# Decay attention with two MLPs on one core: W_out's bounds from VectorE maxima, filler products on TensorE, and a new table of priorities

## The chip, the cores and the metric

The kernel runs on one core of a Trainium2 chip. The metric is the device time of that core in microseconds (us). Engines go by these names: PE is TensorE's matrix products and PEld its weight loads, DVE is VectorE, ACT is ScalarE, POOL is GpSimd, and SP is the queue that issues the DMAs.

## The reference

Three layers follow one another. Attention: 4 batches, 8 heads, 576 positions, head size 64.

```python
scores = scale * (q @ k.T) + cum[:, None] - cum[None, :]   # cum = cumsum(log(clip(f)))
attn = softmax(causal(scores)); x = attn @ v               # then (2304, 512)
x = relu(x @ w_in) ** 2 @ w_out                            # moe: d_ff 2048
out = (silu(x @ w_gate) * (x @ w_val)) @ w_out2            # moe2: d_ff 1536
```

The weights come as 64-bit floats, so each 512-column block of W_in or W_out is 2 MB and is converted on the chip.

## The kernel before

**Staging.** The first 256 rows of each batch ("early") are worked through for all 16 head pairs; batches 0 and 1 keep their products in fp32 on PE (scores L792, transposition L869, mix with V L933). As soon as batch 0 has its eight pieces of x (ACT L968, then DVE L973), the first MLP starts on this tile: `h<-x,i` (L1141) are the products with W_in, `acc<-g,o` (L1209) those with W_out. The first layer of two tiles is done ahead (384 products L1141) before the first L1209. The rest of attention (f16, L945) and the first MLP then interleave; the second MLP (L1404, L1520) closes the program.

**A weight block** (`stage`) is loaded by SP (L362), two ACT operations take its high and low words (L369, L372), DVE joins them (L377). Then a bound is needed from which a power of two is made as its scale. For W_in and W_out (`nm in "io"`) PE multiplies every 128x128 piece of the block with itself (`gram`, L398; 16 products for a block) and DVE takes the row maxima of the sum (`norm`, L403). For the other weights DVE takes the largest magnitude of each piece (`extent`, L406). `scale_of` and `top` spread the largest value over the partitions by PE (L315, L324) and DVE (L319, L294 to L300). With the scale, `split` writes f16 high and low parts (ACT L457, DVE L461). `tables1` (DVE L1085 to L1093) needs the scales of all eight blocks; the squares (ACT L1170) need `tables1`; then come the f16 high part (ACT L1184), the low part (POOL L1187) and the first L1209.

**The order.** Every piece of work is a `Step` with a priority. `Plan.order` puts the steps on a planned clock, per engine always the ready one with the lowest priority number whose buffers are free; the order that it finds is the program order of each engine, so every engine then runs its own list strictly in order. Priorities of the early attention units (`EPRI`), of the batches' V (`VPRI`), of the weight blocks and of their loads (`IPRI`, `ILOAD`, `OPRI`, `OLOAD`), of the second MLP's weights (`GPRI`, `GATE0`) and `FREE` (how many W_in loads don't wait for the first bias load) are tables of numbers. Two PSUM buffers ("hp", tag `h`) are shared by L1141's results, the `top` of V and small products.

Of the kernel before, what the change touches and what calls it, by code (L numbers as in the profile page):

```python
# [8 lines left out]
F32 = mybir.dt.float32  # L9
F32R = mybir.dt.float32r  # L10
F16 = mybir.dt.float16
BF16 = mybir.dt.bfloat16
# [6 lines left out]
PE, ACT, DVE, POOL, SP = "PE", "ACT", "DVE", "POOL", "SP"  # L19
AFTER = {PE: 0.25, ACT: 0.2, DVE: 0.15, POOL: 0.2, SP: 0.0, None: 0.0}  # L20
DMA_ISSUE = 0.45
QUEUE = 8
DMA_LATENCY = 1.8
DMA_RATE = 290e3
LAG1 = 3
# [31 lines left out]
class Plan:  # L57
# [9 lines left out]
    def add(self, eng, us, fn, deps=(), pri=0, take=(), use=(), nbytes=0, order=(), late=0.0):  # L67
        deps, order = ([d for d in ds if d is not None] for ds in (deps, order))
        st = Step(len(self.steps), eng, us, fn, deps, order, pri, take, nbytes)
        st.hot = getattr(fn, "__name__", "") in SHARED[eng] if eng in SHARED else False  # L70
        st.late = late
        for buf in (*take, *use):
            buf.users.append(st)
        self.steps.append(st)
        return st

    def order(self):
# [22 lines left out]
        while left:  # L100
            moved = False
            for e in free:
# [14 lines left out]
                if e == SP:  # L117
                    free[e] = now + st.us
                    if len(landed) >= QUEUE:
                        free[e] = max(free[e], landed[-QUEUE] + 0.1)  # L120
                    dma_free = max(free[e], dma_free) + st.nbytes / DMA_RATE
                    st.done = dma_free + DMA_LATENCY + st.late
                    landed.append(st.done)
# [39 lines left out]
    return 0.1 + n * 0.0021  # L163


GPRI = 900
GATE0 = -2
GATE = 5
EPRI = [-10, 30, 23, 50, 38, 100, 110, 16, 120, 12, 143, 334, 297, 334, 440, 437]
VPRI = [5, 90, 550, 178]  # L170
IPRI, ILOAD = [60, 65, 75, 41], [-15, -17, 10, 40]
OPRI, OLOAD = [128, 113, 177, 290], [115, 132, 180, 126]
VERBOSE = False
WHOLE = 2
SQUARE = 7
FREE = 2
COPY = (ACT, ACT)
ROUNDS = [(0, 1), (8,), (2, 3), (4, 5), (6, 7)]
LAST = ROUNDS[-1]
# [3 lines left out]
def decay_attention_moe_kernel(ctx: ExitStack, tc, q, k, v, f, w1, w2, wg, wv, wo, outT):  # L183
    nc = tc.nc
    P = 128
    B, H, _, S = q.shape
# [5 lines left out]
    NG1 = w1.shape[0]  # L192
    NG2 = wg.shape[0]
# [9 lines left out]
    HN = 2  # L203
# [15 lines left out]
    ps_h = ctx.enter_context(tc.tile_pool(name="ps_h", bufs=HN, space=bass.MemoryType.PSUM))  # L219
# [10 lines left out]
    add = plan.add  # L230
# [6 lines left out]
    def table(name, *shape, dt=F32):  # L237
        return small.tile([P, *shape], dt, tag=name, bufs=1, name=name)
# [3 lines left out]
    ones = table("ones", P, dt=BF16)  # L242
# [2 lines left out]
    XI, XS = table("xi", B + 1), table("xs", B + 1)  # L245
    KX = table("kx", 2, B * NP)
    FY = table("fy", B + 1)
    MT = table("mt", 2 * NG1 + 9 * NG2, dt=BF16)
    NSC = 2 * NG1 + 3 * NG2
    SWI, SWS = table("swi", NSC), table("sws", NSC)  # L250
    ISF, ISG, ISV = (SWI[:, 2 * NG1 + NG2 * n : 2 * NG1 + NG2 * n + NG2] for n in range(3))
# [36 lines left out]
    o3 = add(ACT, 2.0, lambda: nc.scalar.activation(fc[0], fc[0], AF.Ln), [o3], -10, use=[fc_buf])  # L288
    o3 = add(DVE, 1.9, fc_scan, [o3, o2], -10, use=[fc_buf])
    decayed = add(SP, DMA_ISSUE, lambda: nc.sync.dma_start(cum_d, fc[0]), [o3], -10, use=[fc_buf], nbytes=74000)  # L290

    def power(src, c, kk, inv, s, mask=0x7F800000):
        t = small.tile([P, 2], F32, tag="pw", bufs=4, name="pw")
# [54 lines left out]
    def stage(nm, u, places, pri, lpri, deps=(), gates=(), where="hp"):  # L348
        src = SRC[nm]
        c = {"key": (nm, u), "pri": pri, "pieces": [], "bufs": []}  # L350
        g_buf, g_bank = bank(where)
        col = COL[nm] + u
        joined = []
        k0 = 0
        for tag, nb, make, nk in places:
            buf, n = Buf(tag, nb), 512 * nk
            piece = {"ks": slice(k0, k0 + nk), "nk": nk}
            k0 += nk

            def load(piece=piece, make=make, nk=nk):  # L360
                raw = make()
                nc.sync.dma_start(raw.rearrange("p (k n) -> p k n", k=nk), src[u, :, piece["ks"], :].bitcast(I32))  # L362
                words = raw.rearrange("p (n t) -> p n t", t=2)
                piece["lo"], piece["hi"] = words[:, :, 0], words[:, :, 1]
                piece["b"] = raw.bitcast(BF16).rearrange("p (k n t) -> p k n t", k=nk, t=4)[:, :, :, 3]

            def top_half(piece=piece):
                t = piece["hi"].bitcast(F32)
                nc.scalar.activation(t, t, AF.Prelu, scale=2.0**-112, alpha=2.0**32)  # L369

            def low_half(piece=piece):
                nc.scalar.activation(  # L372
                    piece["lo"], piece["lo"].bitcast(U32), AF.Copy, bias=-0.49, scale=2.0**-29 * (1 - 2.0**-9)
                )

            def join(piece=piece):
                nc.vector.scalar_tensor_tensor(  # L377
                    piece["hi"], piece["hi"], 3, piece["lo"], op0=ALU.logical_shift_left, op1=ALU.bitwise_or
                )

            ld = chained(add(SP, DMA_ISSUE, load, deps, lpri + 0.1 * u, take=[buf], nbytes=WIDE * P * n * 8,
                             order=[prev(tag), *gates, *paced(nm), *came[-PACE[nm]:][:1]]), tag)
            s1 = add(ACT, 0.1 + act_us(n), top_half, [ld], pri, use=[buf])
            s2 = add(ACT, 0.1 + act_us(n), low_half, [ld], pri, use=[buf])
            came.append(s1)
            joined.append(add(DVE, dve_us(n), join, [s1, s2], pri, use=[buf]))
            c["pieces"].append(piece)
            c["bufs"].append(buf)
            c["load"] = ld

        def gram(piece):
            for kk in range(4)[piece["ks"]]:
                if kk == 0:
                    c["ps"] = g_bank()
                w = piece["b"][:, kk - piece["ks"].start, :]
                for n in range(4):
                    b = w[:, P * n : P * n + P]
                    nc.tensor.matmul(  # L398
                        c["ps"][:, 0:P], b, b, start=kk == 0 and n == 0, stop=kk == 3 and n == 3,
                    )  # L400

        def norm():
            nc.vector.tensor_reduce(MT[:, col : col + 1], c["ps"][:, 0:P], axis=mybir.AxisListType.X, op=ALU.max)  # L403

        def extent(piece, at):
            nc.vector.tensor_reduce(  # L406
                MT[:, at : at + 1], piece["hi"].bitcast(F32), axis=mybir.AxisListType.X, op=ALU.max,
                apply_absolute_value=True,
            )

        c["joined"] = joined
        if (nm, u) in PEEKED:
            pass
        elif nm in "io":
            st = None
            for piece, buf, jn in zip(c["pieces"], c["bufs"], joined):
                st = add(PE, 0.25 * piece["nk"], lambda piece=piece: gram(piece), [jn, st], pri,
                         take=() if st else [g_buf], use=[buf, *([g_buf] if st else ())])
            c["cols"] = (col, col + 1)
            c["stat"] = [add(DVE, 0.05 + dve_us(P), norm, [st], pri, use=[g_buf])]  # L420
        else:
            m0 = 2 * NG1 + 3 * (col - 2 * NG1)
            c["cols"] = (m0, m0 + len(places))
            c["stat"] = [
                add(DVE, dve_us(512 * piece["nk"]), lambda piece=piece, at=m0 + n: extent(piece, at), [jn], pri, use=[buf])
                for n, (piece, buf, jn) in enumerate(zip(c["pieces"], c["bufs"], joined))
            ]
        return c

    def scale_of(nm, u, c, pri, where="hp"):  # L430
        idx = COL[nm] + u
        kk, mask = (13, 0x7F000000) if nm == "o" else (13 if nm in "gv" else 14, 0x7F800000)
        lo, hi = c["cols"]
        whole = 1 if nm in "io" else 512
        return top(
            lambda: MT[:, lo:hi], hi - lo, c["stat"], pri,
            lambda ps: power(ps, VSCALE * 1.02 * whole, kk, SWI[:, idx : idx + 1], SWS[:, idx : idx + 1], mask), 0.9,
            where=where, square=whole > 1,
        )
# [558 lines left out]

    def own_scale(nm, u, places, pri=GPRI, lpri=GPRI - 5, deps=(), gates=(), where="hp"):
        c = stage(nm, u, places, pri, lpri, deps=deps, gates=gates, where=where)  # L1000
# [15 lines left out]
    def peek(nm, u, places):  # L1016
# [3 lines left out]
        for n, (tag, nb, make, nk) in enumerate(places):  # L1020
# [7 lines left out]
            def extent(n=n):  # L1028
                if "t" not in cell:
# [6 lines left out]

            ld = chained(add(SP, DMA_ISSUE, load, (), GPRI - 4, take=[buf], nbytes=WIDE * P * 4096 * nk,
                             order=[prev(tag), *paced("v"), *came[-1:]]), tag)
            t_buf = stats[0][1] if stats else Buf("pk", 2)
            st = add(DVE, dve_us(512 * nk), extent, [ld, *(s[0] for s in stats[-1:])], GPRI, use=[buf, *([t_buf] if stats else ())],  # L1040
                     take=() if stats else [t_buf])
# [11 lines left out]

        a = add(ACT, 0.3, real, [stats[-1][0]], GPRI, use=[t_buf])
        a = add(DVE, 0.35, shift, [a], GPRI, use=[t_buf])
# [12 lines left out]
    came = [None] * 8  # L1068
    v_batch(0, VPRI[0])
    for n in range(NP):  # L1070
# [578 lines left out]
    order = plan.order()  # L1649
# [60 lines left out]
```

## Time and profile before

| | |
|---|---|
| median of 3 runs | 980.5 us (980.01 to 981.52) |
| profiled execution | 981.62 us, of it 979.8 us span from first to last instruction |
| PE busy | 941.8 us, 96% of the span |
| DVE, ACT, POOL busy | 63%, 62%, 36% |
| granted PE clock, mean | 0.987 |
| first product L1141 | 59.92 us |
| first product L1209 | 130.31 us |

A busy figure is the union of the times in which an engine had an instruction in work. Shares are means over stages that differ: PE's idle time lies mostly in the first 60 us.

### The profile page before, as it was taken

The numbers are of one execution on the slowest core, as the hardware profiler recorded it, in microseconds if no ns is written. First come the engines' busy times: TensorE is split into PE (matmuls) and PEld (weight loads), VectorE is DVE, ScalarE is ACT, GpSimd is POOL, SyncE is SP. The second block draws the span as 40 slices with busy tenths as digits, with TensorE's granted clock in tenths as the row PEclk, the third lists the DMA queues.
The fourth block names the chain that finished last, engine by engine and source line by source line (L and its number), as shares of the span: only waits on it lengthen the run. The fifth ranks groups of instructions, "written<-read, shape, count | busy, mean of one in ns | idle before, by whom it ended". The sixth has DMA issues, their size and how long they took to land. (4 is left out here: it accounts for less than half of the span.)

```text
span 979.8 us, 22430 instructions
## 1 busy us (share of the span) xinstructions
PE 941.8 (96%) x8875; PEld 739.6 (75%) x8875; DVE 615.5 (63%) x1385; ACT 606.7 (62%) x1145; POOL 348.1 (36%) x440
## 2 busy tenths in 40 slices
PE   3899998999999999989999989999999999999998
PEld 1678786887778788767788877777988777777774
DVE  5678757746566677877799999445464363434332
ACT  5789896867778789867787866325453343332232
POOL 1332243354344535434285775113141222210120
PEclk9799999999999999989999999999999999999999
DMA  8795629467787889898962512001101001000101
GB/s 279 230 337 165 152 76 226 106 188 171 144 181 159 184 149 249 178 245 204 259 205 87 203 57 66 1 1 34 56 11 55 2 1 43 1 1 9 36 1 43
DMA packets 147944, 117.46 MB, mean 120 GB/s; under 512 B 98240, under 2 KB 136128, under 8 KB 142592
## 3 DMA queue, kind: packets, MB, share of 16 engines
q1 hardware_dynamic: 147840, 116.04, 45.1%
q8 instruction: 69, 1.13, 0.5%
q14 instruction: 35, 0.29, 0.1%
HBM read 83.44 MB, written 9.51 MB: 95 GB/s over the span
## 5 line engine op out<-in xcount | busy, mean ns | idle before, releaser
L1209 PE MATMUL acc<-g,o 128*128 128x256 f16 x1728 | 209.1, 274 | 0.6 <-POOL g L1187 0.6
L1141 PE MATMUL h<-x,i 128*128 128x256 f16 x1728 | 209.2, 274 | 0.0
L1209 PEld LDWEIGHTS <-o 128*128 128x128 f16 x1728 | 163.7, 98 | 32.7 <-issue 11.8
L1141 PEld LDWEIGHTS <-i 128*128 128x128 f16 x1728 | 164.1, 98 | 29.1 <-issue 8.1
L1520 PE MATMUL acc<-o,f 128*128 128x512 f16 (+1 forms) x720 | 145.7, 358 | 0.5 <-ACT o L1493 0.5
L1520 PEld LDWEIGHTS <-f 128*128 128x128 f16 x720 | 70.0, 98 | 64.5 <-issue 0.8
L776 POOL TENSOR_SCALAR_AFFINE_SELECT bias<-bias 128x128 f32<-128x128 f32 (+1 forms) x160 | 64.4, 412 | 143.0 <-DVE cg L815 77.2
L1483 POOL TENSOR_TENSOR tmp<-tmp,o 128x256 f32<-128x256 f32 (+1 forms) x30 | 23.4, 782 | 246.6 <-ACT o L1477 246.6
L1187 POOL TENSOR_TENSOR g<-tmp,g 128x512 f16<-128x512 f32 x56 | 75.2, 1343 | 95.9 <-ACT g L1184 95.8
L835 ACT ACTIVATE s<-s,cg 128x256 f32<-128x256 f32 (+4 forms) x144 | 83.4, 582 | 15.1 <-DVE cg L815 14.7
L815 DVE CUSTOM_DVE_ANT_0 s<-ps,bias 128x512 f32<-128x512 f32 (+3 forms) x160 | 73.3, 480 | 29.3 <-PE ps L792 23.4
L898 DVE SCALAR_TENSOR_TENSOR p<-s,cg,p 128x512 f16<-128x512 f32 (+4 forms) x112 | 74.2, 679 | 23.0 <-ACT p L894 22.3
L1404 PEld LDWEIGHTS <-g 128*128 128x128 f16 x720 | 65.4, 98 | 10.7 <-issue 2.7
L894 ACT ACTIVATE p<-s,cg 128x512 f16<-128x512 f32 (+4 forms) x112 | 66.9, 616 | 8.6 <-ACT s L835 5.1
L1449 ACT ACTIVATE r<-r,ms 128x768 f32<-128x768 f32 (+1 forms) x30 | 26.1, 870 | 73.9 <-DVE r L1421 73.7
L1404 PEld LDWEIGHTS <-v 128*128 128x128 f16 x720 | 65.4, 98 | 6.5
L1404 PE MATMUL v<-i,g 128*128 128x256 f16 (+1 forms) x540 | 67.9, 262 | 1.8 <-DVE r L1421 1.6
L1404 PE MATMUL v<-i,v 128*128 128x256 f16 (+1 forms) x540 | 67.9, 262 | 0.0
L1421 DVE TENSOR_TENSOR r<-r,h 128x512 f32<-128x512 f32 (+1 forms) x30 | 19.0, 633 | 72.6 <-PE h L1404 68.4
L1487 POOL TENSOR_TENSOR r<-r,o 128x768 f32<-128x768 f32 (+1 forms) x30 | 45.0, 1498 | 42.5 <-ACT o L1480 41.7
L1421 DVE TENSOR_TENSOR r<-r,v 128x512 f32<-128x512 f32 (+1 forms) x60 | 38.0, 633 | 34.1 <-PE v L1404 32.0
L1404 PEld LDWEIGHTS <-eg 128*128 128x128 f16 x540 | 49.3, 98 | 10.7 <-issue 1.8
(185 smaller groups left out, 1626.2 us busy)
## 6 DMA issues: line engine op xcount, KB each, us to landing
raw<-in_moe_w_out_dram SPq DMA_DIRECT2D x11, 1024.0 KB, 6.4
bias<-cum_d SPq DMA_DIRECT2D x16, 576.0 KB, 4.6
raw<-in_moe_w_val_dram SPq DMA_DIRECT2D x9, 1024.0 KB, 5.8
raw<-in_moe_w_gate_dram SPq DMA_DIRECT2D x9, 1024.0 KB, 6.9
raw<-in_moe_w_in_dram SPq DMA_DIRECT2D x8, 1024.0 KB, 6.0
vr<-in_v_dram SPq DMA_DIRECT2D x32, 256.0 KB, 4.3
x_d<-tmp SPq DMA_DIRECT2D x18, 256.0 KB, 3.0
kr<-in_k_dram SPq DMA_DIRECT2D x16, 288.0 KB, 4.1
```

The source lines that it names most:

```text
L776: nc.gpsimd.affine_select(diag, diag, pattern=[[-1, w]], compare_op=ALU.is_ge, fill=-8e9, base=0, channel_multiplier=1)
L815: nc.vector.tensor_tensor_reduce(out=s[r0:r1, n0:e1], in0=c["ps", ti, ci, h][r0:r1, : e1 - n0], in1=c["bias"][r0:r1, h, n0:e1], scale=-0.1 ...
L835: nc.scalar.activation(s[:, :ext], s[:, :ext], AF.Exp, bias=cg[:, mc : mc + 1], scale=-1.0, accum_out=cg[:, 2:3],)
L894: nc.scalar.activation(pv[:, 0, :ext], s[:, :ext], AF.Copy, scale=cg[:, 3:4])
L898: nc.vector.scalar_tensor_tensor(pv[:, 1, :ext], s[:, :ext], cg[:, 3:4], pv[:, 0, :ext], op0=ALU.mult, op1=ALU.subtract,)
L1141: nc.tensor.matmul(HP[key][:, u, :], w[:, wi, kk, c * P : (c + 1) * P], x[:, xi, kk, :], start=(kk == 0 and (wi, xi) == (0, 0)), stop=(kk ...
L1187: nc.gpsimd.tensor_tensor(G[k0][1][:, 1], G[k0][0], G[k0][1][:, 0], op=ALU.subtract)
L1209: nc.tensor.matmul(acc[:, d - part[0], :], w[:, wi, c, d * P : (d + 1) * P], G[k0][1][:, gi, u, :], start=(m == 0 and d == part[0] and (wi ...
L1404: nc.tensor.matmul(R[reg][:, which, :w], t[:, wh, w1_ : w1_ + P], x[:, xh, xi, kk], start=fresh and which == 0 and kk == 0 and (wh, xh) == ...
L1421: nc.vector.tensor_tensor(out(), x(), y(), op=ALU.add)
L1487: nc.gpsimd.tensor_tensor(g, g, R["g"][:, 0, 1:4], op=ALU.subtract)
L1520: nc.tensor.matmul(acc_of(d), wd[:, cc, d * P : (d + 1) * P], R["g"][:, gi, 2 * m : 2 * m + 2].rearrange("p a t -> p (a t)"), start=mm == ...
```

## The change

W_out's blocks now take the branch of `extent`: their bounds are nine DVE maxima over the joined pieces (new line L417), and their Gram products and `norm` are gone. W_in keeps its Gram products. 130 products of a constant tile `ones` with itself, 128x512, whose results nothing reads (`keep_clock`, L295), become PE steps with the highest priority number, so the planner puts one wherever PE would stand idle on its clock; they use the two "hp" buffers. All tables of priorities change. Line numbers grow by 11 behind the new function.

```diff
+WARM = 130
-GPRI = 900
-GATE0 = -2
+GPRI = 895
+GATE0 = -1
-EPRI = [-10, 30, 23, 50, 38, 100, 110, 16, 120, 12, 143, 334, 297, 334, 440, 437]
+EPRI = [84, -11, -1228, -173, 17, 207, 26, -63, 272, 261, 415, 539, 152, 235, -12, -45]
...
-FREE = 2
+FREE = 4
...
+    def keep_clock():
+        ps = ps_h.tile([P, 512], F32, tag="h", name="ps")
+        nc.tensor.matmul(
+            ps.rearrange("p (a n) -> p a n", a=4), ones, ones.unsqueeze(1).to_broadcast([P, 4, P]), start=True, stop=True
+        )
+
+    last = o2
+    for _ in range(WARM):
+        last = add(PE, 0.215, keep_clock, [last] if last is o2 else [], 10**6, take=[Buf("hp", HN)], order=[last])
...
-        elif nm in "io":
+        elif nm == "i":
...
-            m0 = 2 * NG1 + 3 * (col - 2 * NG1)
+            m0 = 2 * NG1 + (9 * NG2 + 4 * u if nm == "o" else 3 * (col - 2 * NG1))
...
-        whole = 1 if nm in "io" else 512
+        whole = 1 if nm == "i" else 512
```

**PE, in the stage before the first L1141.** Before, the list begins with the scores of the first head pair and the first Gram products:

```order
L792 MATMUL ps<-kr,qr 128x256 x2
L398 LDWEIGHTS raw
L398 MATMUL ps<-raw 128x128
L398 LDWEIGHTS raw
L398 MATMUL ps<-raw 128x128
```

Now 48 fillers (L295) stand ahead of everything, and 66 more between the real products up to the first L1152 (the former L1141); this is a piece behind the first eight Gram products (L409):

```order
L409 MATMUL ps<-raw 128x128
L295 LDWEIGHTS ones
L295 MATMUL ps<-ones 128x512
L295 LDWEIGHTS ones
L295 MATMUL ps<-ones 128x512
L803 MATMUL ps<-kr,qr 128x256 x2
L575 LDWEIGHTS ones
L575 MATMUL ps<-vmax,ones 128x4
L295 LDWEIGHTS ones
L295 MATMUL ps<-ones 128x512
```

One filler stands alone in the MLP stage and the last 15 right ahead of the first product with W_out (L1220, the former L1209), behind all 384 products L1152.

**ACT, where batch 0's last pieces of x are made** (L968 before, L979 now; L369 and L372 are W_in's and W_out's words, L835 exponentials). Before:

```order
L835 ACTIVATE s,cg<-s,cg 128x256 x2
L369 ACTIVATE raw<-raw 128x1024
L372 ACTIVATE raw<-raw 128x1024
L835 ACTIVATE s,cg<-s,cg 128x128 x2
L876 COPY PT<-ps 128x512
L876 COPY PT<-ps 128x256
L876 COPY PT<-ps 128x512
L968 ACTIVATE x<-ps,xs 128x128
L369 ACTIVATE raw<-raw 128x1024
L968 ACTIVATE x<-ps,xs 128x128
```

Now:

```order
L380 ACTIVATE raw<-raw 128x1024
L887 COPY PT<-ps 128x256
L383 ACTIVATE raw<-raw 128x1024
L979 ACTIVATE x<-ps,xs 128x128
L887 COPY PT<-ps 128x512
L887 COPY PT<-ps 128x256
L979 ACTIVATE x<-ps,xs 128x128 x2
L380 ACTIVATE raw<-raw 128x1024
L383 ACTIVATE raw<-raw 128x1024
```

Ahead of the eighth piece ACT had 9 rows of L369, 8 of L372 and 20 exponentials; it has 7, 7 and 16 now. The fifth unit's exponentials and the last W_in words stand behind it.

**DVE, ahead of `tables1`** (L1096 on, the former L1085). Now the last W_out maxima stand here, the one of the block whose first piece lies in the buffer `xm` last of all:

```order
L388 SCALAR_TENSOR_TENSOR x_963<-x_963 128x1024
L472 SCALAR_TENSOR_TENSOR o_1713<-raw,sws,o_1713 128x1024 x2
L417 TENSOR_REDUCE mt<-raw 128x1
L417 TENSOR_REDUCE mt<-x_963 128x1
L388 SCALAR_TENSOR_TENSOR xm<-xm 128x512
L826 ISA s,cg<-ps,bias 128x256
L826 ISA cg 128x1
L417 TENSOR_REDUCE mt<-xm 128x1
L330 TENSOR_REDUCE top<-ps 2x1
```

All nine maxima stand ahead of `tables1`, in the place of four `norm` reductions of 128x128. On SP the load into `xm` has moved from ahead of the first DMA transposes to behind the first four of them.

## Rows read from the trace of the kernel before

**Rows 1.** The page, part 1: busy time and share of PE.
```profile
PE 941.8 (96%) x8875; PEld 739.6 (75%) x8875; DVE 615.5 (63%) x1385; ACT 606.7 (62%) x1145; POOL 348.1 (36%) x440
```
**Rows 2.** Stages: PE, PEld, DVE, ACT, POOL busy us (count), clock, DMA share, GB/s.
```profile
0.00:59.90 59.90, 39.53 (x227) 27.67 (x227) 37.77 (x120) 43.29 (x84) 15.23 (x48) 0.89 0.84 272
59.90:130.30 70.40, 68.93 (x605) 55.51 (x604) 55.28 (x185) 62.27 (x135) 20.67 (x44) 1.00 0.58 177
130.30:446.00 315.70, 309.99 (x3439) 247.27 (x3438) 212.80 (x595) 247.70 (x517) 136.02 (x208) 0.98 0.78 177
446.00:979.80 533.80, 523.33 (x4610) 409.13 (x4607) 309.67 (x486) 253.43 (x411) 176.21 (x142) 1.00 0.21 62
```
**Rows 3.** PE's groups, 0 to 59.9 us: busy, mean ns, idle before and releaser.
```profile
L792 PE MATMUL ps<-kr,qr 64*128 64x256 f32 x24 | 9.8, 583 | 9.3 <-DMA qr<-in_q_dram 7.8 <-DVE cg L815 1.4
L398 PE MATMUL ps<-raw 128*128 128x128 bf16 x64 | 8.9, 297 | 6.4 <-DVE raw L377 6.4
```
**Rows 4.** Eight like PE records at three times (timeline), and a stage (as Rows 2).
```profile
24.55 2.07 PE L869 MATMUL ps<-p,s 128*128 128x128 f32 x8
...
41.81 2.07 PE L869 MATMUL ps<-p,s 128*128 128x128 f32 x8
...
73.57 1.06 PE L869 MATMUL ps<-p,s 128*128 128x128 f32 x8
...
40.00:45.00 5.00, 4.98 (x22) 3.42 (x22) 3.89 (x15) 4.40 (x8) 1.87 (x4) 0.50 0.90 295
```
**Rows 5.** PE's timeline: start us, us, line, names, shapes, count.
```profile
75.75 1.10 PE L398 MATMUL ps<-raw 128*128 128x128 bf16 x8
76.68 0.84 PE L1141 MATMUL h<-x,i 128*128 128x256 f16 x6
...
130.31 2.13 PE L1209 MATMUL acc<-g,o 128*128 128x256 f16 x18
...
758.87 5.34 PE L1520 MATMUL acc<-o,f 128*128 128x512 f16 x24
```
**Rows 6.** ACT's groups, 0 to 59 us (columns as Rows 3).
```profile
L369 ACT ACTIVATE raw<-raw 128x1024 f32<-128x1024 f32 x9 | 10.3, 1147 | 12.4 <-DMA raw<-in_moe_w_in_dram 12.4
L372 ACT ACTIVATE raw<-raw 128x1024 int32<-128x1024 uint32 x8 | 9.0, 1129 | 0.0
L835 ACT ACTIVATE s<-s,cg 128x256 f32<-128x256 f32 (+1 forms) x20 | 9.0, 462 | 0.8 <-DVE cg L815 0.8
```
**Rows 7.** DVE's reductions into the table of bounds, whole span (columns as Rows 3).
```profile
L406 DVE TENSOR_REDUCE mt<-raw 128x1 bf16<-128x1024 f32 x8 | 9.7, 1212 | 0.1
...
L403 DVE TENSOR_REDUCE mt<-ps 128x1 bf16<-128x128 f32 x8 | 2.3, 288 | 4.4 <-PE ps L398 4.4
```
**Rows 8.** From `tables1` to the first L1209: DVE, ACT, POOL timelines.
```profile
124.82 0.15 DVE L1093 TENSOR_TENSOR al<-al 128x4 f32<-128x4 f32 x1
...
124.75 0.60 ACT L1163 ACTIVATE hold<-h 128x512 f32<-128x512 f32 x1 [0.64 <-PE h L1141]
125.24 0.76 ACT L457 ACTIVATE o<-x,sws 128x512 f16<-128x512 f32 x1
125.89 1.33 ACT L1170 ACTIVATE hold<-hold,al 128x512 f32<-128x512 f32 x2
127.12 1.13 ACT L1184 CAST g<-hold 128x512 f16<-128x512 f32 x2
...
127.81 2.28 POOL L1187 TENSOR_TENSOR g<-hold,g 128x512 f16<-128x512 f32 x2 [1.77 <-ACT g L1184]
```
**Rows 9.** SP's timeline: the load into `xm` and the first transposes.
```profile
67.47 0.43 SPq L362 DMA_DIRECT2D xm<-in_moe_w_out_dram  x1
...
108.37 3.90 SPq L922 DMA_TRANSPOSE PT<-p  x3
```
**Rows 10.** Two later stages with a lower clock (columns as Rows 2).
```profile
160.00:170.00 10.00, 8.34 (x67) 5.71 (x67) 6.65 (x26) 4.40 (x12) 2.78 (x4) 0.83 1.05 273
...
430.00:440.00 10.00, 9.68 (x88) 6.88 (x86) 7.96 (x24) 6.04 (x13) 2.27 (x7) 0.72 1.12 299
```

More of the change, by code (lines that the diff above doesn't have):

```diff
@@ L163, in pool_us @@
     return 0.1 + n * 0.0021
-GPRI = 900
-GATE0 = -2
+GPRI = 895
+GATE0 = -1
 GATE = 5
-EPRI = [-10, 30, 23, 50, 38, 100, 110, 16, 120, 12, 143, 334, 297, 334, 440, 437]
-VPRI = [5, 90, 550, 178]
-IPRI, ILOAD = [60, 65, 75, 41], [-15, -17, 10, 40]
-OPRI, OLOAD = [128, 113, 177, 290], [115, 132, 180, 126]
+EPRI = [84, -11, -1228, -173, 17, 207, 26, -63, 272, 261, 415, 539, 152, 235, -12, -45]
+VPRI = [11, -292, 536, 601]
+IPRI, ILOAD = [303, -473, 276, 202], [-471, 170, 327, -259]
+OPRI, OLOAD = [279, 410, 340, 342], [-413, 225, 178, 605]
 VERBOSE = False
@@ L247, in decay_attention_moe_kernel @@
     FY = table("fy", B + 1)
-    MT = table("mt", 2 * NG1 + 9 * NG2, dt=BF16)
+    MT = table("mt", 2 * NG1 + 9 * NG2 + 4 * NG1, dt=BF16)
     NSC = 2 * NG1 + 3 * NG2
```

## The prediction

> **What bounds it now.** I read the page's busy shares first, then the stages, then PE's groups and timeline in the first stage, then the other engines' rows where PE waits. The reader is to see that PE has work in 96% of the span [rows 1] and that its missing time is not spread evenly: 59.90 - 39.53 = 20.4 us of it lie ahead of the first MLP product, only 1.5 us between that and the first product with W_out, 5.7 us up to 446 us and 10.5 us in the rest [rows 2]. From the first L1141 at 59.92 on, a product that PE need not do is time gained, and a later start of that stage is time lost. In the first stage PE waits for q (7.8 us) and for joined weights (6.4 us) [rows 3]. It also runs at the lower of its two clock levels, 1.2 GHz: between 40 and 45 us the granted clock is 0.50, and eight records of L869 take 2.07 us there, and at 24.55 us already, against 1.06 us at 2.4 GHz later [rows 4].
>
> **The change, part by part.** The sum is made against the profiled execution (981.62 us, 979.8 of span); it lies 1.1 us over the median of 980.5, so I apply the difference to the median.
>
> *Gram products of W_out.* 64 products, in eight groups of eight, stood between the first L1141 and the first L1209. A group holds PE from 75.75 to 76.68, 0.93 us [rows 5], so 8 x 0.93 = 7.4 us leave PE, where 68.9 of 70.4 us were busy. This is the firmest term. One group of W_in's moves into this stage (+0.93), so 6.5 us leave it.
>
> *Maxima on DVE.* Nine reductions come, seven of 1024 columns at 1.21 us and two of 512 columns, which the trace before doesn't show; they cost between 0.29 (128 columns) and 1.21, I take half of 1.21 [rows 7]. That is 9.7 us, less four L403 at 0.29: 8.5 us net on DVE, all ahead of `tables1`. DVE was busy for 55.3 of the 70.4 us there [rows 2], so there is cover of 15 us, which shrinks as the stage does. DVE loses other rows ahead of `tables1`: 2 of 14 splits, 2 of 10 V maxima, 5 of 13 low parts of p and the rest of one unit, some 8 us, so its list up to there is about as long as before. The 1.21 us for 1024 columns are about one element in 1.2 ns. The Trainium skill (VectorE: DVE Perf Modes, Rules for kernel authors) speaks against the edit: it calls `tensor_reduce` the slowest of VectorE's operations and advises to restructure where it is on the hot path. The rows give the same price; whether that path is hot is the first rival below, and by the rule the time would be the one given there.
>
> *Fillers.* 130 products of 512 columns. The nearest row is L1520's, 24 in 5.34 us, 0.2225 us each [rows 5]; at the low clock about twice that. 114 stand ahead of the first L1152: 25.4 us, and some 2 us more while the first ones still run slowly. They cost nothing where PE would wait (20.4 us before), and where they raise the clock: the 39.5 busy us of the first stage become between 20 (all halved, as L869) and 33 (as L398, whose eight take 0.93 instead of 8 x 8.9/64 = 1.11), and I take 25, since L869, L792 and L933 are three quarters of it. That frees 14.5 us. So 27.4 us of fillers meet 35 us of room. If that cover were gone, what is queued behind a filler, the scores and Gram products, would come late, and ACT and DVE behind them. The clock record disagrees: its mean of 0.89 over the stage [rows 2] would leave only 59.9 x 0.11 = 6.6 us to free, and the third rival would be nearer by 8 us; I go by the 2.07 us at 24.55. The Trainium skill (TensorE: Matmul & The Clock Gate, Seeing it yourself) warns that records of the clock have been unreliable on this chip and wants them checked against other figures; the 2.07 us at 24.55 bears it out.
>
> *The new order up to x.* The first L1141 needs the eighth piece of x. ACT's list ahead of it is shorter by 2 L369 (2 x 1.14), 1 L372 (1.13), 4 exponentials (4 x 0.45) and one copy (some 0.5): 5.7 us [rows 6]. DVE's is shorter by some 4.7 us. ACT was busy for 43.3 of 59.9 us and idle mostly at the start, for W_in's loads (12.4 us), which stay. So the first L1152 comes 5.7 us earlier by ACT's list. The faster scores take away part of ACT's remaining waits for PE; between 0 and 3 us, I take 1.5. First L1152: 59.9 - 7.2 = 52.7 us. PE's own list adds up to 27.4 + some 21.5 (the 25, less a Gram group and a unit's products) = 49 us, so the fillers just fit.
>
> *From there to the first L1220.* 70.4 - 6.5 = 63.9 us; six more products L869 (+1.5) and two fewer score products (-0.4) are on this side now: 65.0. But all 384 L1152 now stand ahead of it, so behind the last one PE waits for its copy (0.60 us), a half block's split (0.76), two squares (1.33), a cast (half of 1.13) and POOL's low part (half of 2.28) [rows 8]: 4.4, with handoffs some 4.7 us, of which the 15 fillers (3.3 us) are a part and no extra. First L1220: 52.7 + 65.0 + 4.7 = 122.4, against 130.3: 7.9 us earlier. Left undone by then are 1.5 us of score products (two of 256 and four of 128 columns), which follow later. Net -6.4 us.
>
> *The rest.* From 446 us on PE's order is the same, so that time moves as it is. Between, the order differs everywhere. PE lost 5.7 us to waits there [rows 2] and 10 x 0.17 + 10 x 0.28 = 4.5 us to a lower clock in two places [rows 10]. Nothing in the lists says that this gets better or worse; I take 0, with ends of -8 and +6.
>
> Sum: 980.5 - 6.4 = 974.1, taken as **974.0 us**; its own range is 969 to 978.5.
>
> **Rivals.** (1) *W_out's bounds come no earlier than now.* `tables1` ended at 124.97 [rows 8]. The load into `xm` went out at 67.47; now it stands behind the first four transposes, which ended at 112.3 [rows 9]. If these come only 3 us earlier, `xm` lands near 115 us, and two ACT operations, the join, the maximum (each half of a row of 1024 columns, some 0.6 [rows 6, 7]) and the `top` steps, some 5 us together, bring `tables1` to 120 us or later; maxima on a full DVE would do the same. PE would then wait at the first L1220 to about 127 to 130: -3 + 1.5, 979 to 982 us, say 980.5. For it speaks that the planner itself put 15 fillers there; against it, that everything ahead of the transposes is earlier. Chance 0.15.
>
> (2) *The middle gets better too.* If the new order also removes most of the 10.2 us of waits and low clock between 130 and 446 us, 8 of them, the time is 966. Chance 0.20.
>
> (3) *The fillers hold PE up* (slower). PE's list is fixed: a filler that doesn't fall into a wait pushes real work. Fillers 28.9 + 2 us less 14.5 freed and 7.4 removed leave +9.0 us against 20.4 + 1.5 = 21.9 us of waits. The change loses as soon as fewer than 9 of those 21.9 us are covered, because the planned waits lie elsewhere than the real ones or because a filler waits for an "hp" buffer that DVE still reads. With 4 covered the time is 985.5. Against it: the wait for q (7.8 us) and the first for joined weights [rows 3] stand just where the 48 leading fillers are, some 12 us. Chance 0.10.
>
> (4) *The clock doesn't rise* by products of a constant. Fillers would take 0.43 us: 114 x 0.43 = 49 us ahead of the first L1152, some 990 us. PE's dense stretch after 60 us ran at 1.00, so I give it 0.03.
>
> **The numbers.** Forecast 0.48, rivals 0.15, 0.20, 0.10, 0.03, and 0.04 for new waits in the middle that eat the gain (980). A difference under 0.2%, 2 us, can't be told from none here. Faster: 0.47 of the 0.48, 0.20, and 0.05 of the first rival: 0.72. Within 0.2%: the other 0.10 of that rival, the 0.04 and 0.01 of the forecast, 0.15. Slower: 0.13. The range from 965 to 982 leaves out (3), (4) and the tail of (2).
>
> **What would show it.** In the new profile the first L1152 should start at 51 to 55 us and the first L1220 at 119 to 125, the granted clock should be at 1.00 from some 5 to 8 us on, eight L880 records should take about 1.06 us before 50 us, DVE's maxima should last 1.21 us each, and from 446 us less 6 on the rows should be those of before. It is wrong if L1152 starts later than 58 us (fillers in the way), if PE stands for more than 6 us before L1220 (bounds late), or if PE's idle time in the middle changes by more than 6 us.

## The result, and the profile after

The changed kernel took 970.28 us (median of 6 runs, 969.19 to 973.41), the kernel before 980.57 us beside it (6 runs, 979.08 to 981.52). The ratio of the mean times is 0.9902, 95% interval 0.9884 to 0.9920: 9.6 us or 1.0% faster (the medians lie 10.3 us apart). The forecast was 974.0 us, range 965 to 982. The profiled execution of the changed kernel took 972.56 us, of it 970.9 us of span.

The stages of the changed kernel, cut at its first L1152 (55.70 us), its first L1220 (123.84 us) and the 24 products L1220 from which PE's order is that of before; columns as in [rows 2]:

```profile
0.00:55.70 55.70, 53.23 (x311) 29.41 (x311) 33.73 (x102) 37.42 (x70) 15.03 (x44) 0.94 0.81 251
55.70:123.84 68.14, 67.25 (x575) 51.50 (x574) 59.00 (x184) 61.94 (x129) 16.41 (x39) 1.00 0.70 209
123.84:434.04 310.20, 307.29 (x3436) 244.25 (x3435) 226.46 (x623) 252.79 (x532) 143.23 (x215) 0.99 0.79 181
434.04:970.90 536.86, 525.10 (x4625) 410.44 (x4622) 310.21 (x488) 255.05 (x416) 177.59 (x143) 1.00 0.21 62
```

The kernel before, cut at the same places of its program:

```profile
0.00:59.92 59.92, 39.55 (x227) 27.67 (x228) 37.77 (x120) 43.31 (x84) 15.23 (x48) 0.89 0.84 272
59.92:130.31 70.39, 68.92 (x605) 55.52 (x604) 55.28 (x185) 62.26 (x135) 20.68 (x44) 1.00 0.58 177
130.31:444.37 314.06, 308.35 (x3425) 245.79 (x3423) 211.38 (x593) 246.14 (x514) 134.97 (x208) 0.98 0.77 177
444.37:979.80 535.43, 524.96 (x4625) 410.60 (x4622) 311.09 (x488) 254.98 (x415) 177.25 (x143) 1.00 0.21 62
```

Line by line the span changes by -4.22, -2.25, -3.86 and +1.43 us, together -8.9 us. PE's idle time in the first stage went from 20.4 us to 2.5 us, yet that stage became only 4.2 us shorter: the fillers are counted as busy.

PE's timeline of the changed kernel at the places of [rows 4], [rows 5] and [rows 8]:

```profile
1.10 12.70 PE L295 MATMUL ps<-ones 128*128 128x512 bf16 x48 [1.10 <-POOL ones L279]
13.81 1.11 PE L409 MATMUL ps<-raw 128*128 128x128 bf16 x8
...
17.95 1.11 PE L409 MATMUL ps<-raw 128*128 128x128 bf16 x8 [1.06 <-DVE raw L388]
...
26.29 1.16 PE L880 MATMUL ps<-p,s 128*128 128x128 f32 x8
...
42.79 1.05 PE L880 MATMUL ps<-p,s 128*128 128x128 f32 x8
...
53.77 1.26 PE L295 MATMUL ps<-ones 128*128 128x512 bf16 x5
54.96 0.70 PE L803 MATMUL ps<-kr,qr 64*128 64x256 f32 x4
...
55.70 1.48 PE L1152 MATMUL h<-x,i 128*128 128x256 f16 x12
...
118.63 1.49 PE L1152 MATMUL h<-x,i 128*128 128x256 f16 x12
119.95 4.05 PE L295 MATMUL ps<-ones 128*128 128x512 bf16 x15
123.84 0.27 PE L1220 MATMUL acc<-g,o 128*128 128x256 f16 x1
125.90 2.34 PE L1220 MATMUL acc<-g,o 128*128 128x256 f16 x20 [1.79 <-POOL g L1198]
```

The eight L880 records take 1.05 to 1.16 us where [rows 4] had 2.07. The record of the granted clock shows 1.00 in the first 26 us with one exception, which follows an idle stretch (PE alone: busy us, count, clock, DMA share, GB/s):

```profile
16.90:19.20 2.30, 1.22 (x9) 0.99 0.96 256
19.20:26.00 6.80, 6.55 (x26) 0.50 0.69 221
```

On DVE the maxima of 1024 columns take 1.21 us as in [rows 7] (the first line below counts other weights' maxima too), one of 512 columns 0.69 us, and `tables1` ends at 120.91 us instead of 124.97 [rows 8]. SP issues the `xm` load right behind the four transposes, which now end at 106.66 us instead of 112.27 [rows 9]:

```profile
L417 DVE TENSOR_REDUCE mt<-raw 128x1 bf16<-128x1024 f32 x14 | 16.9, 1212 | 0.1
```

```profile
114.00 0.69 DVE L417 TENSOR_REDUCE mt<-xm 128x1 bf16<-128x512 f32 x1
...
120.76 0.15 DVE L1104 TENSOR_TENSOR al<-al 128x4 f32<-128x4 f32 x1
```

```profile
102.76 3.90 SPq L933 DMA_TRANSPOSE PT<-p  x3
106.72 0.57 SPq L373 DMA_DIRECT2D xm<-in_moe_w_out_dram  x1
```

### The profile page after: what moved, and what is told of

Read it like the earlier page. It is cut to its first block, busy times and chain, and to the rows that moved or that the text cites. A ratio compares the mean times of both kernels' runs of the same rounds, so it can differ in the third digit from the quotient of the medians.

```text
span 970.9 us, 22565 instructions
## 1 busy us (share of the span) xinstructions
PE 952.9 (98%) x8941; PEld 735.6 (76%) x8941; DVE 629.4 (65%) x1394; ACT 607.2 (63%) x1145; POOL 352.3 (36%) x440
## 5 line engine op out<-in xcount | busy, mean ns | idle before, releaser
L1152 PE MATMUL h<-x,i 128*128 128x256 f16 x1728 | 210.5, 274 | 0.7 <-ACT hold L1174 0.7
L1220 PE MATMUL acc<-g,o 128*128 128x256 f16 x1728 | 208.0, 273 | 1.8 <-POOL g L1198 1.8
L1152 PEld LDWEIGHTS <-i 128*128 128x128 f16 x1728 | 163.1, 98 | 30.7 <-issue 9.6
L1220 PEld LDWEIGHTS <-o 128*128 128x128 f16 x1728 | 163.1, 98 | 29.6 <-issue 8.5
L787 POOL TENSOR_SCALAR_AFFINE_SELECT bias<-bias 128x128 f32<-128x128 f32 (+1 forms) x160 | 68.0, 433 | 122.3 <-DVE cg L826 68.8
L909 DVE SCALAR_TENSOR_TENSOR p<-s,cg,p 128x512 f16<-128x512 f32 (+4 forms) x112 | 77.9, 710 | 25.2 <-ACT p L905 24.5
```

The source lines that it names most:

```text
L787: nc.gpsimd.affine_select(diag, diag, pattern=[[-1, w]], compare_op=ALU.is_ge, fill=-8e9, base=0, channel_multiplier=1)
L909: nc.vector.scalar_tensor_tensor(pv[:, 1, :ext], s[:, :ext], cg[:, 3:4], pv[:, 0, :ext], op0=ALU.mult, op1=ALU.subtract,)
L1152: nc.tensor.matmul(HP[key][:, u, :], w[:, wi, kk, c * P : (c + 1) * P], x[:, xi, kk, :], start=(kk == 0 and (wi, xi) == (0, 0)), stop=(kk ...
L1220: nc.tensor.matmul(acc[:, d - part[0], :], w[:, wi, c, d * P : (d + 1) * P], G[k0][1][:, gi, u, :], start=(m == 0 and d == part[0] and (wi ...
```

## The experiments

Two kinds of edit have to be kept apart. In some runs the order of every engine stays exactly as it was and only single instructions are left out or added (e1 to e5, e9 to e12). In others the planner orders anew (e6 to e8); there one edit moves thousands of instructions.

### The fillers, in the changed kernel's own order

The step stays in the plan, its product is issued or not (shown for e2; e1 has `n < 0`, e3 `n < 114`; e4 issues two products for each `n >= 48`):

```diff
-    for _ in range(WARM):
-        last = add(PE, 0.215, keep_clock, [last] if last is o2 else [], 10**6, take=[Buf("hp", HN)], order=[last])
+    for n in range(WARM):
+        last = add(PE, 0.215, keep_clock if n < 48 else lambda: None, [last] if last is o2 else [], 10**6, take=[Buf("hp", HN)], order=[last])
```

**No fillers (e1).**

> The changed kernel in its own order on every engine, only that the 130 products of ones are not issued. My theory: the fillers stand in waits and pay for themselves by the clock. Without them PE runs its early scores, transpositions and Gram products at 1.2 GHz again (eight L880 records about 2.07 us at 25 us, not 1.05 to 1.16), and the first L1152 comes at 57 to 60 us instead of 55.7; the whole takes 972 to 975 us, 2 to 5 us longer than the changed kernel. Rival A (ACT's shorter list sets the first L1152, PE's clock there is worth nothing): first L1152 within 1 us of 55.7, total 969.5 to 971. Rival B (the fillers hold PE up, since PE is busy 53.2 of 55.7 us): first L1152 at 50 to 53 us, total 965 to 968.

Measured: 973.2 us (971.41 to 974.34, ratio 0.9918, interval 0.9902 to 0.9933), first L1152 at 52.46 us. The total lies where my theory had it, the first L1152 where rival B had it: neither came out whole.

**Only the first 48 (e2).**

> The changed kernel in its own order, only the 48 fillers ahead of the first Gram product are issued, the other 82 are not. My theory: the clock is at 2.4 GHz when the first Gram product runs at 13.8 us but falls back in the waits behind it, as PE then stands idle for some 10 to 15 of the next 40 us; first L1152 at 55 to 58 us, total 970 to 973. If the leading ones carry all of the worth: as the changed kernel or 1 to 3 us better (first L1152 before 54). If they carry none: as without any fillers.

Measured: 972.16 us (ratio 0.9914, 0.9895 to 0.9932), first L1152 at 52.35 us, clock 0.50 from 19 to 26 us and 0.67 from 26 to 35. So the leading fillers' clock does not last, which I had expected, but the first L1152 is not late, which I had not.

**Without the last 15 (e3; the one filler that stands alone in the MLP stage is left out too).**

> The changed kernel in its own order, only the filler in the MLP stage stays out or in as planned and the last 15, ahead of the first L1220, are not issued. My theory: they stand in the serial tail behind the last L1152, where PE would wait; without them PE waits 5 to 6 us there, the first L1220 starts at 123.8 to 126 as now and the total is the same within 1 us (969 to 971.5). Rival: without them the granted clock falls behind the wait and the following products run slow, 2 to 4 us more. The early part of this kernel is that of the changed one: if its clock stays at 1.00 between 19 and 26 us, where it was 0.50 in the profiled execution of the changed kernel, I expect the first L1152 some 3 us earlier, at 52.5 to 53.5 us.

Measured: 969.99 us (969.86 to 972.21, ratio 0.9891, 0.9875 to 0.9907), as my theory had it; the first L1152 came at 54.05 us, later than the 52.5 to 53.5 us that I had given for a clock that stays up. PE's timelines show what the totals hide. First e1, then e3:

```profile
52.46 1.49 PE L1152 MATMUL h<-x,i 128*128 128x256 f16 x12
...
57.60 1.11 PE L409 MATMUL ps<-raw 128*128 128x128 bf16 x8 [1.16 <-DVE raw L388]
...
121.52 0.27 PE L1220 MATMUL acc<-g,o 128*128 128x256 f16 x1 [3.38 <-ACT g L1195]
123.94 4.42 PE L1220 MATMUL acc<-g,o 128*128 128x256 f16 x20 [2.14 <-POOL g L1198]
```

```profile
54.05 1.48 PE L1152 MATMUL h<-x,i 128*128 128x256 f16 x12
...
121.34 0.37 PE L1220 MATMUL acc<-g,o 128*128 128x256 f16 x1 [3.38 <-ACT g L1195]
123.75 4.51 PE L1220 MATMUL acc<-g,o 128*128 128x256 f16 x24 [2.04 <-POOL g L1198]
```

Without fillers the first L1152 comes at 52.46 us, 1.6 us before e3, whose clock stayed at 1.00 in the whole first stage, and 3.2 us before the profiled execution of the changed kernel: the fillers do hold PE up there. By the first L1220 nothing of that is left (121.52 and 121.34 us): e1 gives 1.16 us of its lead back in a wait for joined weights, the second line of its timeline, which e3 doesn't have. So in these two profiles what PE gains ahead of the first L1152 is not gained at the end of the stage. Behind the wait, which the last 15 fillers would fill, both kernels run slowly: e3's 24 products take 4.51 us against 2.78 us for 24 elsewhere, 1.7 us lost, and the granted clock from 124 to 126 us is 0.50 in both and 1.00 in the changed kernel. So the last 15 do something that I had not counted, but the totals don't show it (969.99 us without them, 970.28 us with them). The medians put all fillers together at 2.9 us (973.2 against 970.28), but the ranges overlap. In e1's profile 1.7 us of its loss is a fall of the clock at 424 to 434 us (granted 0.83), which the profiled execution of the changed kernel has as well; whether the early fillers make such falls rarer is not shown.

**The late ones doubled (e4).**

> The changed kernel in its own order, only each of the last 82 fillers is two products (82 more of 0.22 us at full clock: 66 or 67 of them, 15 us, ahead of the first L1152, 15 ahead of the first L1220). My theory: the fillers just fit, with 2.5 us of idle time left in the first stage, so most of the 15 us appear: first L1152 at 64 to 70 us, and the 15 further ones give 3 us where only 1.8 of wait is left; total 978 to 985. Rival (other engines set the pace and PE's list has slack that the profile shows as busy): first L1152 below 60, total below 975.

Measured: 983.65 us (982.23 to 985.77), 13.4 us more than the changed kernel, first L1152 at 67.23 us. The expectation held: 66 more products of 0.2225 us are 14.7 us, and 11.5 us of them came out at the first L1152, or 13.2 us against e3, whose clock stayed up there as e4's did. There is no slack for 66 more fillers.

### Fillers in the order before (e5)

The same `keep_clock`, issued 48 times ahead of PE's list:

```diff
+    add(PE, 0.0, lambda: [keep_clock() for _ in range(48)], [o2], -10**6)
```

> The kernel before in its own order on every engine, with 48 products of ones ahead of PE's list. They end near 13.4 us, so the first scores start there and not at 7.8 us, ahead of the first Gram product as before. My theory, from the run with only the first 48 fillers: the clock falls back in the waits behind them and the gain is small: first L1141 (with its line moved, L1149) at 59 to 61 us, total 979 to 982 us. Rival (the raised clock at the start carries a part of the gain by itself): first such product at 56 to 58, total 975 to 978.

Measured: 981.41 us beside 980.59, ratio 1.0001 (0.9991 to 1.0011); the first MLP product at 59.13 us (59.92 before). No gain from the 48 leading fillers in the old order. But they don't hold the clock there (PE alone, two stretches of the profile):

```profile
20.00:25.00 5.00, 3.70 (x11) 0.50 0.57 215
...
40.00:45.00 5.00, 4.98 (x23) 0.50 0.83 289
```

What a clock held up through the whole first stage would be worth in the old order was not run.

### One part alone, ordered anew (e6 to e8)

> The kernel before with only W_out's bounds taken from DVE maxima (no Gram products of W_out, no fillers, the old tables of priorities; the planner orders anew). My theory: 7.4 us of Gram products leave a stage that PE bounds: first L1209 at 121 to 125 us, total 972 to 976. Rival A (bounds late or DVE full, as in my first rival): first L1209 at 127 to 131, total 979 to 983. Rival B (the gain comes from the new order alone, and the old tables place the maxima badly): total 977 to 980 with PE waiting 4 to 6 us more than before somewhere up to 446 us.

> The kernel before with only the new tables of priorities (Gram products of W_out stay, no fillers). My theory: the tables carry the earlier first stage (first L1141 at 52 to 55 us, by ACT's shorter list) and the 4 to 6 us of the middle, but the Gram products stand in PE's way: total 975 to 979. Rival A (tables carry nearly all): 970 to 973. Rival B (tables suit only the new work): 979.5 or more.

> The changed kernel with W_out's Gram products put back (fillers and new tables stay). My theory: the 7.4 us of products come back into the stage between first L1152 and first L1220, less what the serial tail there hides: total 975 to 978, first L1220 at 128 to 132. Rival (DVE, relieved of 8.5 us of maxima, gives back what PE loses, or the products fill waits): 970 to 973.

Measured: 996.95 us for the maxima with the old tables (ratio 1.0156, 1.0141 to 1.0171), 995.22 us for the new tables alone (1.0140, 1.0124 to 1.0155), 982.45 us for the changed kernel with its Gram products (1.0011, 0.9998 to 1.0023). All three totals missed my theory. e7's lies in its rival B (the tables suit only the new work), which is open upwards; e8's first L1220, at 128.6 us, came where I had it, its total did not, and where it loses the rest was not followed. Much of the time is lost far from the edit. In e6 the longest wait is in the second MLP (waits of PE: total, times, longest), though one of 4.8 us for DVE (`cg`) stands in the edit's own stage, where the first L1209 comes at 131.9 us:

```profile
PE h L1404 <- ACT r L1431: 10.8, 1, 10.8
```

In e7 PE's early list waits for joined weights (18.1 us, against 6.7 us before), and its first L1141 comes at 68.97 us:

```profile
PE ps L398 <- DVE raw L377: 18.1, 5, 13.8
```

So these runs price the planner's new order together with the part. That is why the next two keep the order.

### The Gram products, in a fixed order (e9, e10)

e9 is the old order; where it had a Gram product of W_out there is now the maximum on DVE:

```diff
...
-                st = add(PE, 0.25 * piece["nk"], lambda piece=piece: gram(piece), [jn, st], pri,
+                st = add(PE, 0.25 * piece["nk"], lambda piece=piece, at=o0 + n: gram(piece) if nm == "i" else extent(piece, at), [jn, st], pri,
...
-            c["stat"] = [add(DVE, 0.05 + dve_us(P), norm, [st], pri, use=[g_buf])]
+            c["stat"] = [add(DVE, 0.05 + dve_us(P), norm if nm == "i" else None, [st], pri, use=[g_buf])]
```

> The kernel before in its own order on every engine; at the places of W_out's Gram products the DVE maxima are issued (line L406 on DVE, nothing on PE), and W_out's four row maxima of Gram sums are gone. Old tables, no fillers. My theory: 64 products of 7.4 us leave the stage that PE bounds, but the old order gives tables1 less than that, since DVE's list does not get shorter: first L1209 at 124 to 127 us, total 974.5 to 978. Rival A (tables1 comes no earlier than 124 us, so PE waits in the products' place): first L1209 at 128 to 132, total 979 to 982. Rival B (the whole 7.4 us or more come out): first L1209 at 122.9, total 971 to 974, and the new tables and fillers are worth 1 to 3 us only.

Measured: 979.66 us beside 980.15, ratio 0.9992 (0.9978 to 1.0005). Rival A's numbers came true: no difference. The stage from 60 to 130 us of e9, and below it that of the kernel before (columns as in [rows 2]):

```profile
60.00:130.00 70.00, 63.38 (x545) 48.91 (x544) 64.03 (x195) 61.75 (x135) 18.96 (x44) 1.00 0.60 177
```

```profile
60.00:130.00 70.00, 68.53 (x601) 55.15 (x602) 55.28 (x185) 61.87 (x135) 20.37 (x42) 1.00 0.58 177
```

PE lost 5.2 us of work and gained 5.2 us of idle time; DVE went from 55.28 to 64.03 busy us, 8.75 more. PE now waits for DVE (`cg`, `x`, `vmax`), `tables1` ends at 124.59 us (124.97 before), and the first L1209 comes at 129.65 us. But it is not `tables1` for which PE waits, as rival A had it. All the idle time lies between 60 and 100 us, where PE is busy for 33.38 of 40 us (38.53 before); from 100 to 130 us it works without a break in both kernels, past the end of `tables1`. First e9, then before, then e9's timeline at the end of the stage:

```profile
60.00:100.00 40.00, 33.38 (x289) 25.68 (x287) 35.96 (x98) 33.83 (x65) 9.34 (x25) 1.00 0.63 211
100.00:130.00 30.00, 30.00 (x258) 23.23 (x257) 28.07 (x98) 27.92 (x71) 9.62 (x20) 1.00 0.56 133
```

```profile
60.00:100.00 40.00, 38.53 (x346) 31.71 (x347) 31.84 (x99) 35.63 (x70) 11.97 (x26) 1.00 0.63 210
```

```profile
124.44 0.15 DVE L1093 TENSOR_TENSOR al<-al 128x4 f32<-128x4 f32 x1
```

```profile
129.65 0.60 PE L1209 MATMUL acc<-g,o 128*128 128x256 f16 x4
```

e10 is the changed kernel in its own order, with the 64 Gram products issued too, unread, at each block's last maximum:

```diff
+        def unread(at):
+            if nm == "o" and at == m0 + len(places) - 1:
+                c["ps"] = ps_h.tile([P, 512], F32, tag="h", name="ps")
...
+                            nc.tensor.matmul(c["ps"][:, 0:P], b, b, start=kk == 0 and n == 0, stop=kk == 3 and n == 3)
```

> The changed kernel in its own order, with W_out's 64 Gram products issued as well (at the place of each block's last maximum, into an hp buffer; nothing reads them). My theory: PE bounds the stage between the first L1152 and the first L1220, so the 7.4 us come back nearly whole: last L1152 ends near 127 us instead of 120, total 976 to 978.5. Rival (what ends that stage is W_out's bounds and the chain of squares behind them, so PE has slack there): last L1152 later but the first long run of L1220 at 127 to 129, total 971 to 974.

Measured: 977.39 us (976.91 to 980.97), ratio 0.9975 (0.9965 to 0.9986): 7.1 us more than the changed kernel. Its last products L1152 and first L1220 (lines 10 further on; the profiled execution is the slowest of the eleven):

```profile
126.34 1.48 PE L1162 MATMUL h<-x,i 128*128 128x256 f16 x12
127.67 4.05 PE L295 MATMUL ps<-ones 128*128 128x512 bf16 x15
131.55 0.27 PE L1230 MATMUL acc<-g,o 128*128 128x256 f16 x1
```

They stand 7.7 us behind those of the changed kernel (118.63 and 123.84 us), with the first L1152 at 55.39 us and PE idle for 1.0 us between: it is the products' own time that comes back. The same 64 products, exchanged for the maxima, are worth 0.5 us in the old order, which can't be told from nothing; left out beside the maxima, they are worth 7.1 us in the new one. What remains of the gain in e10, 2.8 us of 980.15, is that of the new order and the fillers together, net of the maxima. The old order with neither the products nor the maxima was not run.

### The end of the stage, and a steadier version (e11, e12)

In the changed kernel POOL's two masks stand ahead of the first low parts, for which PE waits:

```profile
123.22 1.51 POOL L787 TENSOR_SCALAR_AFFINE_SELECT bias<-bias 128x128 f32<-128x128 f32 x2 [7.01 <-DMA bias<-cum_d]
124.70 2.28 POOL L1198 TENSOR_TENSOR g<-hold,g 128x512 f16<-128x512 f32 x2
```

e11 moves them behind, and leaves all else in place:

```diff
     order = plan.order()
+    names = [getattr(st.fn, "__name__", "") for st in order]
+    lo = [k for k, n in enumerate(names) if n == "g_lo"][:2]
+    early = [st for st, n in zip(order[lo[0] - 40 : lo[0]], names[lo[0] - 40 : lo[0]]) if n == "mask"][-2:]
+    for st in early:
+        order.remove(st)
+    order[lo[1] - 1 : lo[1] - 1] = early
```

> The changed kernel in its own order, only POOL's two masks (L787, 1.5 us) that stand just ahead of the first two low parts (L1198) come behind them. My theory: POOL's list delays the first low part by what is left of the masks when the cast is ready, 1.0 to 1.4 us, and PE waits for just that: the wait ahead of the second product L1220 falls from 1.8 to about 0.6 us, total 1 us less than the changed kernel (968.5 to 969.7). Rival (the masks then come late for DVE's scores, or the wait is given back in the middle): 970 to 971.5, with the wait gone and a new one further on.

Measured: 970.34 us (ratio 0.9900, 0.9882 to 0.9917), as the changed kernel, so the 1 us of my theory is not shown. PE's wait there fell only from 1.79 to 1.28 us, and POOL's first low part then waits for ACT's cast (L1195); half a microsecond is below what these runs can tell.

e12 adds to e11 four fillers in the gap ahead of the second Gram group, where PE stood for 1.06 us:

```diff
-    for _ in range(WARM):
-        last = add(PE, 0.215, keep_clock, [last] if last is o2 else [], 10**6, take=[Buf("hp", HN)], order=[last])
+    for n in range(WARM):
+        last = add(PE, 0.215, keep_clock if n != 51 else lambda: [keep_clock() for _ in range(5)], [last] if last is o2 else [], 10**6, take=[Buf("hp", HN)], order=[last])
```

> The changed kernel in its own order with POOL's two masks behind the first low parts (as in the run before), and four more products of ones (0.9 us) just ahead of the second group of eight Gram products, where PE stood idle for 1.06 us at 16.9 us and the granted clock fell to 0.50 two us later. My theory: with that gap filled the clock no longer falls there, the first L1152 comes at 54.0 to 54.4 us in every execution, the mean clock is 0.998 or more; total 968.3 to 969.5. Rival (that fall has another cause, or only moves to the next gap): mean clock 0.994 to 0.998 as now, first L1152 at 55 or later in the profile, total 970 to 971.

Measured: 969.77 us (5 runs, 968.99 to 970.05, ratio 0.9883, 0.9865 to 0.9902). The mean clock was 0.998 to 1.000 in all five executions; in the six of the changed kernel it was 0.995 to 1.000. PE's stretches from 17 to 26 us of the profiled one (busy us, count, clock, DMA share, GB/s):

```profile
17.00:19.00 2.00, 1.78 (x9) 1.00 0.97 234
19.00:21.00 2.00, 1.72 (x12) 1.00 0.94 373
21.00:26.00 5.00, 5.00 (x33) 1.00 0.44 134
```

The first L1152 came at 54.21 us there, as expected; the total is 0.3 us above the range of my theory. This is the fastest median of all, and the five executions lie closer together than the changed kernel's six, but its interval overlaps that of the changed kernel, so it is not shown to be faster.

## Why the prediction was right, and where not

The time (974.0 against 970.28 us) and the sign were right, and so was the main mechanism, PE's time for the Gram products. That the sum came as near as it did is in part luck: against the forecast the steps below are off by +3.0, -1.6, -5.4 and +1.4 us, which cancel to -2.5. The steps:

| step | predicted | profiled execution |
|---|---|---|
| first L1152 | 52.7 us | 55.70 us |
| from there to the first L1220 | 69.7 us | 68.14 us, 70.20 to its long run |
| from there to where the order is the same | 314.06 + 1.5 us | 310.20 us |
| the rest | 0 | +1.43 us |
| sum | -6.4 us | -8.9 us |

**First L1152: ACT's 52.7 us came out without the fillers, not with them.** "so the fillers just fit" is the sentence that failed. Without late fillers the first L1152 comes at 52.35 to 52.46 us (e2, e1), near the 52.7 us of ACT's shorter list; that this list sets it is not shown, since in e1 ACT waits for PE (0.48 us, for L944) ahead of the last pieces of x. The fillers cost 1.6 us of that where the clock stays up (e3), and 3.2 us in the profiled execution, where it fell; that is just outside the 51 to 55 us which were to show the forecast. In e3 PE was busy for 51.03 of 54.05 us: by its timeline 27.7 us of fillers, near the 27.4 forecast, but 23.3 us of other work, not 21.5, and 3.0 us of waits, which the 49 us of "PE's own list" left out. As e1 and e3 meet again at the first L1220, no run shows that this delay reaches the total. The place is seen in the timeline: five fillers and the scores stand from 53.77 us, right ahead of the first L1152. This is rival 3's mechanism, small; e4 shows that it bites at once when there are more of them. The stage of e3 (columns as in [rows 2]):

```profile
0.00:54.05 54.05, 51.03 (x311) 28.97 (x312) 34.16 (x102) 36.82 (x71) 12.86 (x44) 1.00 0.84 261
```

**The Gram products: right size, wrong word.** "This is the firmest term" treated the 7.4 us as a gain by itself. e10 measures 7.1 us, so the size was right in the new order. In the old order, with the maxima in their place, it is nothing (e9): DVE is busy for 64.03 of 70 us, and PE waits for its scores and V's maxima. That is near the second half of rival 1 ("maxima on a full DVE"), though the waits are not at the first product with W_out, where the rival had them. The rule cited with the maxima (the Trainium skill, VectorE: DVE Perf Modes, Rules for kernel authors) is borne out by e9: the reduction stands on a hot path and gives 979.7 us, as by the rule. In the changed kernel it is not borne out: the maxima bring 8.7 us by their rows (seven of 1.21 and two of 0.69 and 0.70 us, less four L403), near the 8.5 predicted, and yet DVE's work up to the end of `tables1` is 89.80 us, against 88.49 before and 96.65 in e9 (all engines as in [rows 2]; before, e9, the changed kernel):

```profile
0.00:124.97 124.97, 103.13 (x782) 78.65 (x783) 88.49 (x293) 100.23 (x209) 32.68 (x86) 0.95 0.73 230
...
0.00:124.59 124.59, 96.81 (x721) 71.30 (x722) 96.65 (x302) 99.44 (x209) 30.34 (x86) 0.95 0.74 230
...
0.00:120.91 120.91, 117.61 (x872) 79.76 (x873) 89.80 (x281) 96.43 (x194) 30.82 (x82) 0.97 0.76 232
```

So "about as long as before" was right, and it goes with the part of the change that makes the other part pay: the new order puts other DVE work behind `tables1` (226.46 us in the stage from the first L1220 on, against 211.38). That this alone makes the difference between e9 and e10 is argued, not shown: the two orders differ on every engine.

**From the last L1152 to L1220: 4.7 us was about right.** In e3, without fillers, it is 3.4 us to the first product and 5.8 us to the long run. `tables1` (120.91 us) and the copy of the last L1152 (ACT, from 120.49 us) came together, so neither W_out's bounds nor PE's list alone sets that end. They also hang together: the last `top` product that `tables1` needs (L335, at 118.52 us) stands in PE's list among the products L1152, so a longer list makes the bounds late too. Rival 1 had `tables1` at 120 us or later, which came true; its price did not follow, as the last L1152 itself ended at 120.1 us. The load into `xm` was harmless, as the transposes ahead of it ended 5.6 us earlier. The 15 fillers were "a part and no extra", which is right within 0.4 us (3.7 us from the last L1152 to the first L1220, against 3.4 us in e3), but they also hold the clock for the products behind.

**The middle: taken as 0, measured -3.9 us.** PE's idle time there went from 5.71 to 2.91 us. The wait of 2.0 us for `vmax` near 161 us and the clock's fall behind it [rows 10] are gone. That is half of rival 2. But one execution of before overstates it: in the profiles of e5 and e9, which have the old order, this stretch took 311.2 and 311.1 us, with the clock at 1.00 in the ten us around 160, instead of 314.06. Against these the changed kernel's 310.20 us is 1 us better, and 308.22 us in e12 is 3. The stretch behind 434 us came out 1.43 us longer; the same products take 535.43 us in the profile of before and 537.5 us in those of e5 and e12, so it varies by that much between executions.

**The clock.** From 4.9 us on the leading fillers run at full speed, as predicted (5 to 8 us). The fourth rival fell. The granted clock of "1.00 from some 5 to 8 us on" failed for 19.2 to 26 us. Of the six executions, the three with a mean clock of 0.998 or more took 969.19 to 969.95 us, the other three 970.60 to 973.41 us.

## What to carry to other kernels

Work taken off the busiest engine is gained only if the order lets that engine use it: test it once with every engine's order held fixed, in the old order and in the new, since the two answers here were 0.5 and 7.1 us. An edit that goes back through a planner prices the whole new order, and two of the three such runs came out 15 and 16 us slower than the kernel before, in part for reasons far from the edit. Fillers that keep the clock belong into real gaps, above all ahead of a long dense stretch (e3: 1.7 us on 24 products, in the profile); where PE's list is already the limit, each costs about its full time (e4: 13.2 us for 66).

## What the runs showed of the hardware

The clock row can say 1.00 where PE is at its lower level. In the changed kernel the leading fillers take 607 to 634 ns each up to 4.9 us and 376 ns later (min, median and max of the records in two stretches), so by these lines they follow each other at some 0.42 us and then at some 0.22 us, and the row shows 1.00 for both:

```profile
L295 PE MATMUL ps<-ones x10: 607/634/634, 1.1 to 4.9; 128*128 128x512 bf16 x10
...
L295 PE MATMUL ps<-ones x27: 376/376/377, 7.8 to 13.4; 128*128 128x512 bf16 x27
```

The Trainium skill (TensorE: Matmul & The Clock Gate, Seeing it yourself) warns that records of the clock have been unreliable, and this trace agrees.

The same idle gap does not always bring the clock down. With PE idle for 1.06 us near 17 us, the clock fell to 0.50 some one to two us later in the profiles of the changed kernel and of e11, and stayed at 1.00 in that of e3. With the gap filled it stayed up in the profile of e12, and the mean clock was 0.998 or more in all its five executions.
